# Sigmoid attention and a GELU feed-forward on one core: five decoder steps, sums ahead of a small read, parking tiles in the long-lived pool, a later x load

## The chip, the cores and the metric

The kernel runs on one core of one Trainium2 chip, as one program in one launch. The metric is the device time of that launch in microseconds, the median of three executions. TensorE (PE) multiplies, VectorE (DVE) and ScalarE (ACT) do the elementwise work, GpSimd (POOL) and SyncE (SP) issue DMA transfers, each in its own queue and in program order.

## The reference

The feed-forward's input is attention's output. Attention has 8 batches and 12 heads, a sequence of 448 and a head width of 64; the feed-forward is 3584 tokens, 768 to 2048 to 768.

```python
scores = scale * np.matmul(q, k.transpose(0, 1, 3, 2)) - np.log(S)
attn = 1.0 / (1.0 + np.exp(-scores))
out = np.matmul(attn, v)
...
h = x @ w_in
g = 0.5 * h * (1.0 + erf(h * inv_sqrt2))
return (g @ w_out).astype(np.float32)
```

q, k, v are float32. The weights w_in and w_out are drawn as float64 and reach the kernel as 64-bit words, so that the kernel itself makes float32 of them.

## The kernel before

**Attention** is a loop over 24 units `u`: 3 groups of two head pairs (four heads) for each of 8 batches. A unit makes its scores (six `sc` tiles and a tail), a sigmoid on ScalarE (`a`), and the values' product into one PSUM tile `pav` (function `values`). q and k are split into a rounded part and a remainder (`hi`, `lo`), three matmuls for a product. Half-way through `values`, VectorE makes a small read of `pav` (`mark`, L457), and the matmuls that come next into `pav` wait for that read. After it `meanwhile()` runs, and when the unit's values are complete `park` (L469) copies `pav` into an SBUF tile `x`, so that the PSUM banks can be used by the next unit's scores. Units 0 to 5 (the first two batches) store `x` by DMA into four SBUF tiles `x0`, the others into a DRAM scratch `scr_x`. The tile `x` belongs to the pool `at`, which lives as long as attention does.

**The decoder** (class `Decoder`) makes float32 of the weights, in 28 chunks: 16 of w_in, 12 of w_out. A chunk is loaded into `raw`, scaled by two ScalarE passes (L138, L141), finished by three VectorE instructions (L157, L160, L163) in `end`, and after every second chunk `post` makes the Strassen-Winograd sums: four of them for w_in (`mix`, L107 to L110) and seven stores to `scr_in`, or two for w_out (L182, L183) and five stores to `scr_out`. `work` is a generator in three steps a chunk: scale; end and the next load; post. Units 2 to 9, 11 to 18 and 20 to 23 take one step ahead of `values` and two in `meanwhile`. The rest of w_out is decoded in the first feed-forward layer of the first pair of batches.

**The feed-forward** takes the batches in four pairs `b`. `ffn1` has 56 products `n` (7 Winograd products times 8 blocks, 9 matmuls each), `ffn2` has 28 (18 matmuls each). The `late` pool opens when `at` closes and lies in the same SBUF space, so its first tiles (`h2`, `t4`, the `g` slots) must wait until the tiles of `at` are done with. Weight halves are staged by SP (`wst`), rounded on ScalarE (L265) and given a remainder by VectorE (L272). `X0_WORK` lists the products after which the first pair's own x operands are made. In `ffn2` of the first pair, each second product runs `mix_store(i)`: VectorE subtracts twice (`combine`, shown as L588), POOL stores two parts to `scr_out` and then loads the parts for `i+2` (L835) into one of two `wd` tiles; there are six such rounds. At product 4 of `ffn2`, POOL also gets eight loads of the next pair's x (L297).

Of the kernel before, what the change touches and what calls it, by code (L numbers as in the profile page):

```python
# [17 lines left out]
P = 128  # L18
# [4 lines left out]
def tile_sigmoid_attention_gelu_ffn(  # L23
# [88 lines left out]

    def square(m):
        return m.rearrange("p (h f n) -> p h f n", h=2, f=2)

    class Decoder:
        def __init__(self):
            self.raws, self.parts, self.out = {}, {}, None
            self.done = self.groups = self.closed = 0
            self.mixing, self.pending, self.pool = [], [], None  # L120
            self.steps = self.work()
            self.taken = 0
# [10 lines left out]
        def scale(self, i):  # L133
            w = CHUNKS[i][1]
            me = sb.tile([P, KC * S], U32, tag="me", name=f"me{i}", bufs=2)
            self.parts[i] = top = me[:, :w]
            half = self.raws[i].bitcast(I16)[:, : 4 * w].rearrange("p (n t) -> p n t", t=4)
            nc.scalar.activation(  # L138
                top.bitcast(F32), half[:, :, 2], AF.Prelu, bias=-LEAST, scale=-1.0, alpha=TINY
            )  # L140
            nc.scalar.activation(  # L141
# [8 lines left out]
        def end(self, i):  # L150
            _, w, kind, group, at = CHUNKS[i]
            words = self.raws.pop(i)[:, : 2 * w].rearrange("p (n t) -> p n t", t=2)[:, :, 0]
            top = self.parts.pop(i)
            if at == 0:
                self.out = sb.tile([P, 4 * QUAD], F32, tag="wd", name=f"wd{i}", bufs=2)
            bits = self.out[:, at : at + w].bitcast(U32)
            nc.vector.scalar_tensor_tensor(  # L157
                bits, words, 13, top, op0=ALU.logical_shift_right, op1=ALU.bitwise_or
# [3 lines left out]
            )  # L162
            nc.vector.tensor_tensor(bits, bits, words, op=ALU.add)  # L163
            if at:
                (self.mixing if kind == "in" else self.pending).append((group, self.out))

        def post(self):
            while self.mixing:
# [9 lines left out]
            while self.pool and self.pending:  # L178
                (c, e), a = self.pending.pop(0)
                a11, a12, a21, a22 = (a[:, i * QUAD : i * QUAD + QUAD] for i in range(4))  # L180
                s2 = self.pool(f"s{c}_{e}")
# [4 lines left out]
                self.groups += 1  # L186

        def work(self):
# [17 lines left out]
        def to(self, steps):  # L206
            self.go(max(0, math.ceil(steps) - self.taken))
# [4 lines left out]
        def until(self, *need):  # L212
            while not self.has(*need):
                assert self.taken <= 3 * len(CHUNKS)
# [4 lines left out]
    STEPS = {u: (1, 2) for u in (*range(2, 10), *range(11, 19), *range(20, 24))}  # L219
# [100 lines left out]
    def attention(at, ps):  # L320
        raws, vals, parts, probs, pavs, xs = {}, {}, {}, {}, {}, {}
# [51 lines left out]

        def spare(at, name):
            t = at.tile([P, 2, S], F32R, tag="hi", name=name, bufs=3)
            return t.bitcast(F32).rearrange("p a s -> p (a s)")[:, :QUAD]
# [87 lines left out]
        def park(u, p):  # L464
            if u < 0:
                return
            if p == 0:
                xs[u] = at.tile([P, 2, S], F32, tag="x", name=f"x{u}", bufs=2)
            nc.vector.tensor_copy(xs[u][:, p], pavs[u][:, p])  # L469
            b, n = divmod(u, NU)  # L470
            if b < 2:
                j, c = divmod(2 * n + p, KC)
                for i in range(2):
                    dst = x0[j, i].bitcast(F32)[:, c, b * HT : b * HT + HT]
                    nc.gpsimd.dma_start(dst, xs[u][:, p, i * HT : i * HT + HT])
            elif p == 1:
                nc.gpsimd.dma_start(scr_x[:, 2 * n : 2 * n + 2, b * S : (b + 1) * S], xs.pop(u))
# [16 lines left out]
        for u in range(total):  # L494
# [10 lines left out]
            if u == total - 1:  # L505
                W.low_to(3)
                dec.pool = lambda name: spare(at, name)

            def meanwhile():
# [4 lines left out]
                if u == total - 1:  # L514
                    dec.pool = None
                if u == 10:
                    x01, x11, x00 = (x0[jk].bitcast(F32) for jk in ((0, 1), (1, 1), (0, 0)))
                    nc.vector.tensor_tensor(x01, x11, x01, op=ALU.subtract)
                    nc.vector.tensor_tensor(x6, x01, x00, op=ALU.add)
                if u == 19:  # L520
                    lo = x0[0, 0]
# [374 lines left out]
```

## Time and profile before

| | |
|---|---|
| median of 3 runs | 1065.76 us (1063.42 to 1066.15) |
| the profiled execution | 1064.18 us, its span 1062.1 us |
| PE busy | 1014.5 us, 96% of the span |
| DVE busy | 708.0 us, 67% |
| ACT busy | 681.2 us, 64% |
| POOL busy | 120.2 us, 11% |
| mean granted TensorE clock | 0.987 of full speed |
| DMA over the span | 194 GB/s |

The span runs from the first to the last instruction of the profiled execution; some 2 us of the device time lie outside it. Of PE a busy share says little by itself: what counts is where it waited and at which of its two clock levels it ran.

### The profile page before, as it was taken

The numbers are of one execution on the slowest core, as the hardware profiler recorded it, in microseconds if no ns is written. First come the engines' busy times: TensorE is split into PE (matmuls) and PEld (weight loads), VectorE is DVE, ScalarE is ACT, GpSimd is POOL, SyncE is SP. The second block draws the span as 40 slices with busy tenths as digits, with TensorE's granted clock in tenths as the row PEclk, the third lists the DMA queues.
The fourth block names the chain that finished last, engine by engine and source line by source line (L and its number), as shares of the span: only waits on it lengthen the run. The fifth ranks groups of instructions, "written<-read, shape, count | busy, mean of one in ns | idle before, by whom it ended". The sixth has DMA issues, their size and how long they took to land.

```text
span 1062.1 us, 16574 instructions
## 1 busy us (share of the span) xinstructions
PE 1014.5 (96%) x6406; PEld 910.0 (86%) x6406; DVE 708.0 (67%) x822; ACT 681.2 (64%) x935; POOL 120.2 (11%) x186
## 2 busy tenths in 40 slices
PE   9999999899599995999999999999999999999998
PEld 5655555555589995999999999999999999999998
DVE  3667676767577894867338886843688674368874
ACT  5877777776678664556666564676656557666653
POOL 1332121302121225101000000100000000000000
PEclk9999999999899998899999999999999999999999
DMA  9999899997686667656443444643444453334442
GB/s 278 298 334 314 281 303 322 311 323 232 210 303 223 196 196 254 215 161 207 140 133 107 134 145 139 201 158 119 131 127 141 143 169 122 116 98 129 136 141 67
DMA packets 85294, 205.94 MB, mean 194 GB/s; under 512 B 9760, under 2 KB 34624, under 8 KB 85216
## 3 DMA queue, kind: packets, MB, share of 16 engines
q1 hardware_dynamic: 71056, 158.53, 49.1%
q0 software_dynamic: 13856, 46.02, 12.2%
q8 instruction: 50, 0.82, 0.3%
q10 hardware_dynamic: 304, 0.34, 0.1%
q14 instruction: 28, 0.23, 0.1%
HBM read 160.82 MB, written 41.29 MB: 190 GB/s over the span
## 4 chain that ended last, share of the span: by engine, by line
PE 59%; DMA 2%; issue 1%; DVE 0%; POOL 0%; ACT 0%; SPq 0%; DVEq 0%; POOLq 0%; ACTq 0%
PE pf L548 59%; DMA scr_out<-a 1%; DMA a<-scr_out 1%; DVE whl L272 0%; POOL a L835 0%; DMA out_dram<-tmp 0%; DVE a L588 0%; DVE op L588 0%; ACT tmp L803 0%; ACT tmp L798 0%; SPq L747 0%; DVEq L588 0%; DVEq L272 0%; ACTq L798 0%; POOLq L835 0%
## 5 line engine op out<-in xcount | busy, mean ns | idle before, releaser
L548 PE MATMUL pf<-op,whl 128*128 128x448 f32 x2016 | 385.6, 355 | 11.2 <-DVE op L588 11.2
L548 PEld LDWEIGHTS pf<-op,whl 128*128 128x128 f32 x2016 | 383.4, 191 | 12.7 <-DVE op L588 11.9
L548 PE MATMUL pf<-xh_p,whl 128*128 128x448 f32 x1296 | 354.6, 354 | 3.8 <-ACT g L698 2.1
L265 ACT CAST whl<-wst 128x768 fp32r<-128x768 f32 x224 | 186.6, 833 | 216.1 <-PE pf L548 191.0
L272 DVE TENSOR_TENSOR whl<-wst,whl 128x768 fp32r<-128x768 f32 x224 | 213.5, 955 | 141.1 <-ACT whl L265 140.8
L548 PEld LDWEIGHTS pf<-xh_p,whl 128*128 128x128 f32 x1296 | 246.1, 190 | 5.6 <-ACT g L698 2.4
L548 PE MATMUL pf<-xl_p,whl 128*128 128x448 f32 x600 | 212.3, 354 | 0.0
L371 ACT ACTIVATE a<-sc 128x896 f32<-128x896 f32 x144 | 120.3, 927 | 44.2 <-PE sc L397 44.0
L430 PE MATMUL pav<-a,v 64*64 64x448 f32 x1296 | 132.4, 541 | 0.0
L588 DVE TENSOR_TENSOR op<-g,op 128x896 fp32r<-128x896 f32 x112 | 121.4, 1085 | 0.9 <-ACT op L598 0.9
L548 PEld LDWEIGHTS pf<-xl_p,whl 128*128 128x128 f32 x600 | 114.1, 190 | 0.2
L430 PEld LDWEIGHTS pav<-a,v 64*64 64x64 f32 x1296 | 52.2, 132 | 64.0 <-issue 40.7
L598 ACT CAST op<-g 128x896 fp32r<-128x896 f32 x112 | 104.8, 935 | 2.6 <-PE pf L548 2.6
L588 DVE TENSOR_TENSOR g<-g,g 128x896 f32<-128x896 f32 x64 | 69.4, 1085 | 0.0
L397 PE MATMUL sc<-lo,hi 64*128 64x448 f32 x276 | 53.0, 375 | 15.6 <-DVE x L469 15.6
L588 DVE TENSOR_TENSOR tmp<-pf,g 128x448 f32<-128x448 f32 x64 | 40.0, 625 | 31.8 <-PE pf L548 31.2
L397 PEld LDWEIGHTS sc<-lo,hi 64*128 64x128 f32 x276 | 27.1, 186 | 35.5 <-issue 31.5
L585 ACT ACTIVATE g<-tmp 128x448 f32<-128x448 f32 x64 | 40.2, 628 | 25.9 <-DVE tmp L588 25.7
L297 POOL DMA_DIRECT2D x<-scr_x x24 | 17.9, 756 | 299.0 <-ACT g L694 186.1
L363 DVE TENSOR_TENSOR lo<-qk,hi 128x896 fp32r<-128x896 f32 x46 | 50.1, 1089 | 1.1
L457 DVE COPY ones<-pav 128x2 f32<-128x2 f32 x23 | 3.7, 160 | 70.5 <-PE pav L430 70.5
L397 PE MATMUL sc<-hi,lo 64*128 64x448 f32 x276 | 49.8, 349 | 0.0
(75 smaller groups left out, 830.9 us busy)
## 6 DMA issues: line engine op xcount, KB each, us to landing
wst<-scr_in SPq DMA_DIRECT2D x112, 384.0 KB, 3.3
wst<-scr_out SPq DMA_DIRECT2D x112, 384.0 KB, 3.1
v<-v_dram SPq DMA_DIRECT2D x48, 256.0 KB, 8.3
raw<-w_in_dram SPq DMA_DIRECT2D x16, 767.8 KB, 5.5
raw<-w_out_dram SPq DMA_DIRECT2D x12, 1023.5 KB, 6.2
qk<-q_dram SPq DMA_DIRECT2D x23, 448.0 KB, 10.1
qk<-k_dram SPq DMA_DIRECT2D x46, 224.0 KB, 10.6
out_dram<-tmp SPq DMA_DIRECT2D x43, 224.0 KB, 2.1
```

The lines of the kernel that those rows point to most:

```text
L265: nc.scalar.copy(hl[:, 0], t)
L272: nc.vector.tensor_tensor(hl[:, 1], t, hl[:, 0], op=ALU.subtract)
L297: queue.dma_start(dst[:, :, a], src[:, :, a])
L363: nc.vector.tensor_tensor(lo, raw, hi, op=ALU.subtract)
L371: nc.scalar.activation(to, sc, AF.Sigmoid, bias=NEG_LOG_S, scale=SCALE)
L397: nc.tensor.matmul(sc[:, j], ks[rows(j), 1, keys], braid(qs[rows(j), 0]) if braided else qs[rows(j), 0], start=n == 0, stop=n == last,)
L430: nc.tensor.matmul(pav[rows(j), p], vals[u][half, p, j, c], a[p][half, j], start=not swap and c == order[0], stop=c == (order[-1], FULL - ...
L457: nc.vector.tensor_copy(mark, pav[:, :, 0])
L548: nc.tensor.matmul(bank, a, braid(m), **flags)
L585: nc.scalar.activation(straight(dst), unbraid(src), AF.Gelu)
L588: nc.vector.tensor_tensor(out, a, b, op=op)
L598: nc.scalar.copy(op[:, 0], src)
```

## The change

It has five parts.

The decoder now has five steps for a chunk: the first ScalarE pass (`scale`); the second (`place`); `post` for the chunk before; the first two VectorE instructions (`join`); the third one and the next load (`round`). Units 2 to 9 and 11 to 18 take three steps ahead of `values` and two in `meanwhile`, so that `post`, with w_in's four sums, stands ahead of the small read `mark`. Units 20 to 23 take (3,1), (4,1), (4,1) and (4,2) steps.

Two sets of VectorE passes over the first x tiles (at units 10 and 19) also move from `meanwhile` to a place ahead of `values`, and the last remainder of attention's weights moves from the start of unit 23 into its `meanwhile`.

`park` copies each half into its own tile `piece` of the pool `sb`, with three buffers, in the ring that the feed-forward's `tmp` tiles use; it stores each half by itself. `at` holds no parking tile any more. w_out's sums take their scratch from the same ring, so they no longer need a pool lent to them.

In the first feed-forward layer the decoder's steps go to the products 2 to 45 that are not in `X0_WORK`.

In `ffn2` of the first pair the next pair's x is loaded at product 13, not 4; the other pairs keep product 4.

```diff
+    def piece(name):
+        return sb.tile([P, QUAD], F32, tag="tmp", name=name, bufs=3)
...
-            while self.pool and self.pending:
+            while self.pending:
                 (c, e), a = self.pending.pop(0)
                 a11, a12, a21, a22 = (a[:, i * QUAD : i * QUAD + QUAD] for i in range(4))
-                s2 = self.pool(f"s{c}_{e}")
+                s2 = piece(f"s{c}_{e}")
...
             for i in range(len(CHUNKS)):
                 self.scale(i)
-                yield
-                self.end(i)
-                self.load(i + 3)
-                yield
-                self.post()
-                yield
+                yield True
+                self.place(i)
+                yield True
+                yield self.post()
+                self.join(i)
+                yield True
+                self.round(i)
+                yield True
+            yield self.post()
...
-    STEPS = {u: (1, 2) for u in (*range(2, 10), *range(11, 19), *range(20, 24))}
+    STEPS = {u: (3, 2) for u in (*range(2, 10), *range(11, 19))}
+    STEPS |= {20: (3, 1), 21: (4, 1), 22: (4, 1), 23: (4, 2)}
...
-            if p == 0:
-                xs[u] = at.tile([P, 2, S], F32, tag="x", name=f"x{u}", bufs=2)
-            nc.vector.tensor_copy(xs[u][:, p], pavs[u][:, p])
+            x = piece(f"x{u}_{p}")[:, :S]
+            nc.vector.tensor_copy(x, pavs[u][:, p])
...
-            elif p == 1:
-                nc.gpsimd.dma_start(scr_x[:, 2 * n : 2 * n + 2, b * S : (b + 1) * S], xs.pop(u))
+            else:
+                nc.gpsimd.dma_start(scr_x[:, 2 * n + p, b * S : (b + 1) * S], x)
...
-                    dec.to(done + (3 * len(CHUNKS) + 1 - done) * min(1, n / 42))
+                    if n in live:
+                        share = (live.index(n) + 1) / len(live)
+                        dec.to(math.ceil(done + (STEPS_IN_ALL - done) * share))
...
-                if b + 1 < NB and n == 4:
+                if b + 1 < NB and n == (4 if b else 13):
```

On VectorE, inside attention: the end of one unit before (`wd` is a decoded chunk pair, `sin` w_in's sums, `x` the parking tile).

```order
L157 SCALAR_TENSOR_TENSOR wd_718<-raw_467,me_819 128x768
L160 TENSOR_SCALAR raw_467<-raw_467 128x768
L163 ISA wd_718<-raw_467,wd_718 128x1536
L107 TENSOR_TENSOR sin_845<-wd_718 128x384
L108 TENSOR_TENSOR sin_845<-sin_845,wd_718 128x384
L109 TENSOR_TENSOR sin_845<-wd_718 128x384
L110 TENSOR_TENSOR sin_845<-wd_718,sin_845 128x384
L469 COPY x_879<-pav_822 128x448 x2
```

And the unit after it in the changed kernel, where L399 and L390 are the splits of the next unit's q and k, L489 is the small read and L500 the parking copy.

```order
L399 TENSOR_TENSOR lo_0_858<-qk_680,hi_0_857 128x896
L390 CAST hi_1_942<-qk_680 128x896
L399 TENSOR_TENSOR lo_1_943<-qk_680,hi_1_942 128x896
L107 TENSOR_TENSOR sin_949<-wd_722 128x384
L108 TENSOR_TENSOR sin_949<-sin_949,wd_722 128x384
L109 TENSOR_TENSOR sin_949<-wd_722 128x384
L110 TENSOR_TENSOR sin_949<-wd_722,sin_949 128x384
L489 COPY ones<-pav_961 128x2
L171 SCALAR_TENSOR_TENSOR wd_979<-raw_591,me_946 128x768
L179 TENSOR_SCALAR raw_591<-raw_591 128x768
L186 ISA wd_979<-raw_591,wd_979 128x1536
L500 COPY x_0_1007<-pav_961 128x448
```

The four sums stood between the decode and the parking copy; they now stand between the splits and the small read, one unit later.

On VectorE, at the end of attention and the first instructions of the feed-forward, before (L182, L183 are w_out's sums, the two L588 make `t4` and the remainder of `h2`).

```order
L163 ISA wd_2935<-raw_2703,wd_2935 128x2048
L182 TENSOR_TENSOR wd_2699<-wd_2699 128x512
L183 TENSOR_TENSOR s_0_3051<-wd_2699 128x512
L182 TENSOR_TENSOR wd_2935<-wd_2935 128x512
L183 TENSOR_TENSOR s_1_3059<-wd_2935 128x512
L469 COPY x_3067<-pav_3029 128x448 x2
L588 TENSOR_TENSOR x_1_3088<-x_10_110,x_p_114 128x1344
L588 TENSOR_TENSOR x_10_110<-x_10_110,x_0_3087 128x1344
L272 TENSOR_TENSOR whl_3109<-wst_2610,whl_3109 128x768
```

The same place now (L308 is the weights' remainder, L611 are the two former L588).

```order
L186 ISA wd_2981<-raw_2829,wd_2981 128x2048
L308 TENSOR_TENSOR whl_2994<-wst_2630,whl_2994 128x768
L500 COPY x_0_3099<-pav_3074 128x448
L500 COPY x_1_3102<-pav_3074 128x448
L611 TENSOR_TENSOR x_1_3122<-x_10_110,x_p_114 128x1344
L611 TENSOR_TENSOR x_10_110<-x_10_110,x_0_3121 128x1344
L308 TENSOR_TENSOR whl_3143<-wst_2632,whl_3143 128x768
L308 TENSOR_TENSOR whl_3166<-wst_2855,whl_3166 128x768
```

The four sums have left this place (one pair went to unit 22, one into the feed-forward), and one remainder pass has come in.

On POOL, in `ffn2` of the first pair, before (`a` are the mix tiles: L842 stores, L835 loads; L297 loads x).

```order
L842 DMA scr_out_0_99<-a_3983 512x1x128
L842 DMA scr_out_0_107<-a_3983 512x1x128
L835 DMA a_4127<-scr_out_1_98 128x4x128
L835 DMA a_4127<-scr_out_1_102 128x4x128
L835 DMA a_4127<-scr_out_1_106 128x4x128
L297 DMA x_00_4161<-scr_x 128x3x224 x2
L297 DMA x_01_4164<-scr_x 128x3x224 x2
L297 DMA x_11_4167<-scr_x 128x3x224 x2
L297 DMA x_10_4170<-scr_x 128x3x224 x2
L842 DMA scr_out_0_99<-a_4064 512x1x128
L842 DMA scr_out_0_107<-a_4064 512x1x128
L835 DMA a_4204<-scr_out_1_98 128x4x128
```

The end of the six rounds now (L866 stores, L859 loads, L333 loads x).

```order
L866 DMA scr_out_1_108<-a_4169 512x1x128
L859 DMA a_4299<-scr_out_1_98 128x4x128
L859 DMA a_4299<-scr_out_1_102 128x4x128
L859 DMA a_4299<-scr_out_1_106 128x4x128
L866 DMA scr_out_1_100<-a_4234 512x1x128
L866 DMA scr_out_1_108<-a_4234 512x1x128
L866 DMA scr_out_1_100<-a_4299 512x1x128
L866 DMA scr_out_1_108<-a_4299 512x1x128
L333 DMA x_00_4488<-scr_x 128x3x224 x2
L333 DMA x_01_4491<-scr_x 128x3x224 x2
L333 DMA x_11_4494<-scr_x 128x3x224 x2
L333 DMA x_10_4497<-scr_x 128x3x224 x2
```

The eight x loads stood in the middle of the rounds and now stand behind the last store.

## Rows read from the trace of the kernel before

**Rows 1.** Waits of PE, whole span: total us, times, longest.

```profile
PE sc L397 <- DVE x L469: 15.6, 11, 1.7
PE pf L548 <- ACT g L694: 12.4, 1, 12.4
PE pf L548 <- DVE op L588: 11.2, 2, 10.1
PE pf L548 <- ACT g L698: 2.1, 1, 2.1
PE pf L548 <- ACT g L700: 1.7, 1, 1.7
```

**Rows 2.** Windows of PE alone: stretch; length, busy (instructions), granted clock, DMA.

```profile
486.12:676.11 189.99, 189.99 (x1006) 1.00 0.48 146
278.00:284.00 6.00, 5.91 (x23) 0.73 0.21 67
307.00:314.00 7.00, 6.50 (x25) 0.76 0.70 223
425.00:434.00 9.00, 8.71 (x30) 0.64 0.89 303
```

**Rows 3.** Timeline of DVE in attention: start, length, instruction [idle before <- releaser].

```profile
86.60 0.16 DVE L457 COPY ones<-pav 128x2 f32<-128x2 f32 x1 [2.95 <-PE pav L430]
...
89.80 0.56 DVE L107 TENSOR_TENSOR sin<-wd 128x384 f32<-128x384 f32 x1
...
91.81 1.15 DVE L469 COPY x<-pav 128x448 f32<-128x448 f32 x2
...
247.14 0.16 DVE L457 COPY ones<-pav 128x2 f32<-128x2 f32 x1 [2.03 <-PE pav L430]
```

**Rows 4.** Waits of PE's weight loads, attention: total us, times, longest.

```profile
PEld pav L430 <- DVE ones L457: 6.9, 23, 0.3
```

**Rows 5.** Windows of attention: length, busy by engine, granted clock, DMA share, GB/s.

```profile
20.00:80.00 60.00, 56.68 (x576) 33.20 (x574) 38.12 (x58) 46.57 (x56) 20.24 (x36) 1.00 1.03 322
...
200.00:220.00 20.00, 18.35 (x188) 10.19 (x187) 13.59 (x22) 11.94 (x15) 4.09 (x7) 1.00 1.02 357
```

**Rows 6.** Line L477, the parking stores of units 6 to 23, 448 KB each.

```profile
DMA to landing us min/median/max: 6.5/8.1/9.5
```

**Rows 7.** Timeline of ACT, DVE and PE where attention ends.

```profile
274.06 1.31 ACT L846 CAST x<-x 128x1344 fp32r<-128x1344 f32 x1 [15.69 <-DMA scr_x<-x]
261.53 0.68 DVE L182 TENSOR_TENSOR wd<-wd 128x512 f32<-128x512 f32 x1
...
264.26 1.15 DVE L469 COPY x<-pav 128x448 f32<-128x448 f32 x2
274.03 1.56 DVE L588 TENSOR_TENSOR x<-x,x_p 128x1344 f32<-128x1344 f32 x1 [8.62 <-DMA scr_x<-x]
278.09 3.52 PE L548 MATMUL pf<-x,whl 128*128 128x448 f32 x9 [12.41 <-ACT g L694]
```

**Rows 8.** Page, costliest groups: count, busy us, mean ns, idle ahead.

```profile
L272 DVE TENSOR_TENSOR whl<-wst,whl 128x768 fp32r<-128x768 f32 x224 | 213.5, 955 | 141.1 <-ACT whl L265 140.8
```

**Rows 9.** Timeline of POOL in the first pair's second layer.

```profile
389.87 1.52 POOL L842 DMA_DIRECT2D scr_out<-a  x2
397.66 2.26 POOL L835 DMA_DIRECT2D a<-scr_out  x3 [6.27 <-issue]
399.91 5.96 POOL L297 DMA_DIRECT2D x<-scr_x  x8
...
416.41 2.26 POOL L835 DMA_DIRECT2D a<-scr_out  x3 [8.29 <-DMA scr_out<-a]
...
423.78 2.27 POOL L835 DMA_DIRECT2D a<-scr_out  x3 [3.60 <-issue]
```

**Rows 10.** Timeline of DVE there: the fourth and fifth mix.

```profile
404.92 1.29 DVE L588 TENSOR_TENSOR a<-a 128x512 f32<-128x512 f32 x2 [3.69 <-DMA a<-scr_out]
...
422.07 1.29 DVE L588 TENSOR_TENSOR a<-a 128x512 f32<-128x512 f32 x2 [10.12 <-DMA a<-scr_out]
```

More of the change, by code (lines that the diff above doesn't have):

```diff
@@ L135, in scale, with place @@
             me = sb.tile([P, KC * S], U32, tag="me", name=f"me{i}", bufs=2)
-            self.parts[i] = top = me[:, :w]
+            self.parts[i] = me[:, :w]
             half = self.raws[i].bitcast(I16)[:, : 4 * w].rearrange("p (n t) -> p n t", t=4)
             nc.scalar.activation(
-                top.bitcast(F32), half[:, :, 2], AF.Prelu, bias=-LEAST, scale=-1.0, alpha=TINY
-            )
+                self.parts[i].bitcast(F32),
+                half[:, :, 2],
+                AF.Prelu,
+                bias=-LEAST,
+                scale=-1.0,
+                alpha=TINY,
+            )
+        def place(self, i):
+            top = self.parts[i]
             nc.scalar.activation(
@@ L148, in scale, with words @@
             )
-        def end(self, i):
+        def words(self, i):
             _, w, kind, group, at = CHUNKS[i]
-            words = self.raws.pop(i)[:, : 2 * w].rearrange("p (n t) -> p n t", t=2)[:, :, 0]
-            top = self.parts.pop(i)
             if at == 0:
@@ L162, in end, with round @@
             )
+            self.rest[i] = bits, words
+        def round(self, i):
+            bits, words = self.rest.pop(i)
             nc.vector.tensor_tensor(bits, bits, words, op=ALU.add)
+            _, _, kind, group, at = CHUNKS[i]
             if at:
                 (self.mixing if kind == "in" else self.pending).append((group, self.out))
+            self.raws.pop(i)
+            self.load(i + 3)
         def post(self):
+            some = bool(self.mixing or self.pending)
             while self.mixing:
@@ L186, in post @@
                 self.groups += 1
+            return some
         def work(self):
@@ L206, in to @@
         def to(self, steps):
-            self.go(max(0, math.ceil(steps) - self.taken))
+            while self.taken < min(steps, STEPS_IN_ALL):
+                self.taken += 1
+                if not next(self.steps, None):
+                    steps += 1
         def has(self, *need):
@@ L213, in until @@
             while not self.has(*need):
-                assert self.taken <= 3 * len(CHUNKS)
+                assert self.taken <= STEPS_IN_ALL
                 self.go(1)
@@ L563, in tmp @@
             return piece(f"tmp{count['tmp']}")[:, :S]
-        def piece(name):
-            return late.tile([P, QUAD], F32, tag="tmp", name=name, bufs=3)
         def flush():
@@ L674, in ffn1 @@
             done = dec.taken
+            live = [n for n in range(2, 46) if IN_ORDER[n] not in X0_WORK]
             for n, (p, j) in enumerate(IN_ORDER):
```

46 lines of the change are left out of this document (23 added, 23 removed).

## The prediction, as it was put on record

> **What bounds the kernel now.** I read PE's waits over the whole span first [rows 1]. PE is the engine on which the end hangs: once the first pair of batches is done it never stops, and a pair takes 189.99 us for 1008 matmuls, 0.1885 us each, at full clock [rows 2]. So only what PE loses ahead of that can be won back. The list has five entries, and they fall into three places. In attention PE waits 15.6 us in 11 pieces for the parking copy. Where attention ends it waits once, 12.4 us. In the first pair's two layers it waits 2.1 and 1.7 us for ScalarE copies in the first and 11.2 us for VectorE in the second.
>
> Then I read the granted clock behind those waits, in windows of PE [rows 2]: after the 12.4 us wait PE runs at the lower of its two levels for a while (mean 0.73 of full speed over 6 us, so 6 × 0.27 = 1.6 us lost), after the 2.1 us wait likewise (7 × 0.24 = 1.7 us), and after the longest wait of the second layer (9 × 0.36 = 3.2 us). Waits and clock together are 15.6 + 12.4 + 1.6 + 3.8 + 1.7 + 11.2 + 3.2 = 49.5 us. With all of it gone the span would be 1062.1 - 49.5 = 1012.6 us.
>
> **Part one, the sums ahead of the small read.** In a unit with w_in's sums, VectorE does the small read at 86.60, decodes, begins the sums at 89.80 and can park only at 91.81: the four sums hold the parking copy back by 2.0 us [rows 3]. PE then waits up to 1.7 us for the bank [rows 1]. Now the sums run ahead of the small read, where VectorE sat idle 2.95 us until PE had got that far [rows 3]. 2.0 fits into 2.95. The parking copy comes 2.0 us earlier, which is more than the longest of the waits, so these waits go. In units 20 to 22 the third decode instruction moves into the next unit in the same way.
>
> What hides the sums is that idle time, and it is smaller in the last units: 2.03 us at 247.14 [rows 3], where one decode instruction and two w_out sums (about 1.2 + 1.4 us, taken as the row at 261.53 and its like) now stand. There the small read comes some 0.6 us late. PE's weight loads do wait for that read, at all 23 units, 0.3 us at the longest today [rows 4]; so one unit pays up to 0.6 us. I take 0.3.
>
> Two costs are not in the trace. First, the unit becomes shorter while its bytes stay. Attention ends near 278.09 - 12.41 - 27 × 0.1885 = 260.6 us [rows 7, 2], 10.9 us a unit; without the waits 10.2. The transfers ran at 322 GB/s with a DMA share of 1.03 from 20 to 80 us, and at 357 GB/s with 1.02 from 200 to 220 [rows 5]. The shorter unit needs 322 × 260.6 / 245 = 343 GB/s. That lies between the two rows. If 322 is what those kinds of transfer can reach, nearly none of the 15.6 us is won; if 357 is, all. Nothing waits for a load today (no DMA stands in rows 1), and loads are issued one to three units ahead, which covers a deficit for some units. I take 1.0 us.
>
> Second, the parking ring. The copy of a unit's second half reuses the tile of the previous unit's first half; between the two copies lie 10.2 + 0.6 us, of which 0.7 go by until the store is issued. So a store must land within about 10 us. Stores of twice the size landed in 6.5, 8.1 at the median and 9.5 us at most [rows 6]. It holds, but not by much. I take 0.3 us, between nothing and some 0.5 us in each of 20 units. The Trainium skill prices such a transfer differently (DMA: Bandwidth & Descriptors, section Anatomy of one DMA — SWDGE (gpsimd) path: about 2.0 us fixed plus bytes over 436 GB/s). By that the half would land in 2.5 us, an estimate from the page, the whole in 3.1, and the ring could never be late; the trace's 8.1 us for the whole says otherwise, and I follow the trace.
>
> Part one: -15.6 + 0.3 + 1.0 + 0.3 = **-14.0 us**.
>
> **Part two, the end of attention.** ScalarE stood 15.69 us and VectorE 8.62 us until the last parking store had landed, since the feed-forward's first tiles lie where the parking tile of `at` lay [rows 7]. With the tile outside `at` that wait has no object. The next thing late is found by adding up. PE runs out of work at 278.09 - 12.41 = 265.7. ScalarE needs 278.09 - 274.06 = 4.0 us from its copy of `h2` to the `g` copy for which PE waits; it can begin when attention's last matmul is done, near 260.6, and is done by 264.6. VectorE parked at 264.26, after four sums that began at 261.53 [rows 7]. Those 2.7 us are gone, and one remainder pass (0.96 us [rows 8]) has come in: parking begins at 262.5 and ends at 263.6. Then come `t4` and the remainder of `h2`, 1.56 us each: 266.8. So VectorE is late next, by 1.1 us. That is less than the waits of up to 1.7 us behind which the clock stayed at 1.00 [rows 1, 5].
>
> Part two: -12.4 - 1.6 + 1.1 = **-12.9 us**.
>
> **Part three, the decoder's steps in the first layer.** The number of ScalarE and VectorE instructions stays the same, but no step falls on a product with x work any more. The two waits of 2.1 and 1.7 us [rows 1] were for ScalarE copies. Whether they stood behind such a pile I take from the code's order alone; and one pair of w_out sums more lies here now. Bounds: nothing gained, or 3.8 + 1.7 = 5.5 us. I take the middle: **-2.7 us**.
>
> **Part four, x later.** At 399.91 POOL issues eight x loads, 5.96 us of issue time, ahead of the next mix store, and their bytes then compete with it: the load behind that store goes out only at 416.41 [rows 9]. VectorE waits 10.12 us for it [rows 10] and PE 10.1 [rows 1]. With the loads behind the last round this goes. But POOL's own chain stays: a store, its landing, the next load. From one load's issue to the next it took 2.26 + (397.66 - 389.87) = 10.0 us, and later, with little else in flight, 423.78 - 416.41 = 7.4 us [rows 9]. VectorE wants a mix every 36 matmuls, 6.8 us. So the chain is slower than its consumer, and something stays.
>
> The load of round four goes out at 397.66 either way; the next two at 405.1 to 407.7 and 412.4 to 417.7. From a load's first issue to VectorE's start there passed 422.07 - 416.41 = 5.7 us [rows 9, 10]. So the mixes can start at 403.4, at 410.8 to 413.4 and at 418.1 to 423.4. Without waits VectorE would come to them at 404.92 - 3.69 = 401.2, 408.0 and 414.8 [rows 10]. The largest delay is 3.3 to 8.6 us. PE has a reserve: VectorE's 3.69 + 10.12 = 13.8 us of waiting cost PE 11.2, so 2.6 us are covered. PE loses 0.7 to 6.0 us, say 3.4, and 0.6 of clock (between none and 1.7). The x loads themselves have until the second layer's end, over 40 us after product 13 (13 × 18 × 0.1885 = 44).
>
> Part four: -11.2 - 3.2 + 3.4 + 0.6 = **-10.4 us**.
>
> **Sum.** -14.0 - 12.9 - 2.7 - 10.4 = -40.0. The profiled execution's span goes from 1062.1 to 1022.1; 2.1 us lie around it (1064.18 - 1062.1), so 1024.2. That execution lay 1.6 us under the median of the runs, within their spread of 2.7. I predict **1025 us**.
>
> **Rivals.**
>
> *The transfers bound attention.* For it: the DMA share of 1.03 over 60 us [rows 5]. Against it: 357 GB/s in another stretch, and no wait of PE for a load. If 322 GB/s is the ceiling, the unit stays at 10.9 us and part one gives perhaps 2 us: 1025 + 12 = 1037.
>
> *The mix chain, with its slow rounds, takes back most of part four.* For it: the 10.0 us round [rows 9]. Should each round take 10 us and the first layer give nothing either, 1025 + 2.6 + 1.1 + 2.7 = 1031.
>
> *The parking ring (the other side).* Stores land later as units get shorter, VectorE stands in the second half's copy, and PE waits for the bank as before, in every unit and not in 11. It begins to cost when a store takes over 10 us; slower than before it gets when some 23 units lose 1.8 us each (41 us), that is, when half-size stores take about 12 us all the time, against 9.5 at most for whole ones [rows 6]. At 11.5 us each, 23 × 1.5 = 34 us come back: 1059. At 12.2, about 1075.
>
> *The small read is late.* If the sums did not fit in 2.95 us, PE would stand at the second half of `values` and the 15.6 us would only change their place: 1025 + 14 = 1039. The fit of 2.0 into 2.95 speaks against it.
>
> **How the numbers follow.** Forecast 0.72, its own range 1016 (49.5 us less and 2.1 around it give 1014.7) to 1033 (all bounds against me: 1.3 more in attention, 2.7 in the first layer, 3.7 in the second). Transfers as the bound 0.11; the mix chain 0.09; the small read 0.04; the parking ring 0.04, of which half is slower than before. The range 1015 to 1037 leaves out the small read, the ring and part of the transfers' case, under 2 in 10. A measurement of this kernel tells no change from one of 0.3%, 3.2 us. Only the ring's case reaches that: faster 0.96, same 0.02, slower 0.02.
>
> **What would show it.** Right: no entry of some 15 us for the parking copy among PE's waits; ScalarE's first feed-forward copy near attention's last matmul; PE's first wait there near 1 us, with the clock at 1.00; in the second layer a wait of 1 to 6 us for VectorE and mix loads 7 to 10 us apart; x loads after the last mix store. Wrong: PE's weight loads waiting over 0.3 us for the small read in every unit; the parking copy waiting for a store; loads landing late with a DMA share above 1.03 and a rate no higher than 322; new ScalarE waits in the first layer.

## The result, and the profile after

The changed kernel takes 1022.45 us (median of three, 1020.52 to 1023.74) against 1065.76: a ratio of 0.9597 with a 95% interval of 0.9565 to 0.963. The forecast was 1025, with 1015 to 1037 around it. The profiled execution spans 1020.7 us against 1062.1, 41.4 us less. One execution of those that follow, of the whole of e7, took 1774.46 us at a granted clock of 0.556 and is left out of every comparison.

PE's waits over the whole span, after (engine, line, what is waited for: us in total, times, longest); they answer to [rows 1].

```profile
PE pf L574 <- DVE op L611: 5.6, 3, 3.2
PE pf L574 <- DVE x L611: 1.6, 1, 1.6
PE pf L574 <- ACT g L722: 0.8, 1, 0.8
PE sc L429 <- DMA qk<-k_dram: 0.3, 1, 0.3
PE sc L429 <- DVE x L500: 0.3, 1, 0.3
```

Of the eleven waits for the parking copy (now L500) one is left, of 0.3 us. The 12.4 us at the end of attention became 1.6. In the second layer 5.6 us of 11.2 stay. The places where PE passes from one stage to the next tell what each part was worth: its first feed-forward matmul starts at 242.64 us, before at 260.30 (17.7 us earlier); the first layer takes 98.6 us, before 115.7 (17.1 less); the first pair's second layer 103.4, before 110.1 (6.7 less). 17.7 + 17.1 + 6.7 = 41.5, the whole gain. How it splits is a matter of the execution too: in a second profiled one (e0 below) the same three gains are 15.6, 17.1 and 7.6 us.

**Attention.** VectorE's timeline, one unit of the changed kernel (start, length, line, operation; in brackets the idle time before it and what ended it), beside [rows 3]:

```profile
69.81 0.55 DVE L107 TENSOR_TENSOR sin<-wd 128x384 f32<-128x384 f32 x1
...
71.34 0.55 DVE L110 TENSOR_TENSOR sin<-wd,sin 128x384 f32<-128x384 f32 x1
72.80 0.16 DVE L489 COPY ones<-pav 128x2 f32<-128x2 f32 x1 [0.91 <-PE pav L462]
73.43 0.96 DVE L171 SCALAR_TENSOR_TENSOR wd<-raw,me 128x768 uint32<-128x768 uint32 x1 [0.46 <-ACT me L152]
...
75.89 1.15 DVE L500 COPY x<-pav 128x448 f32<-128x448 f32 x2
```

The sums took up 2.0 us of the idle time ahead of the small read L489, of which 0.91 us is left, and the parking copy comes 3.1 us after the small read and not 5.2. The windows of the same kernel (stretch, length, busy time of each engine with its count, granted clock, DMA share, GB/s), beside [rows 5]:

```profile
40.00:80.00 40.00, 40.00 (x410) 24.69 (x412) 29.75 (x45) 34.20 (x42) 15.65 (x29) 1.00 1.02 340
160.00:200.00 40.00, 40.00 (x412) 24.70 (x411) 30.87 (x45) 31.00 (x38) 10.36 (x18) 1.00 1.02 350
```

PE has no gap, and the transfers run at 340 to 350 GB/s with the same share of 1.02.

**The end of attention.** From the timelines of ScalarE, VectorE and PE, beside [rows 7]:

```profile
242.75 1.32 ACT L870 CAST x<-x 128x1344 fp32r<-128x1344 f32 x1 [1.32 <-DMA raw<-w_out_dram]
245.47 1.15 DVE L500 COPY x<-pav 128x448 f32<-128x448 f32 x2
246.53 1.55 DVE L611 TENSOR_TENSOR x<-x,x_p 128x1344 f32<-128x1344 f32 x1
248.19 1.56 DVE L611 TENSOR_TENSOR x<-x,x 128x1344 fp32r<-128x1344 f32 x1
249.80 1.78 PE L574 MATMUL pf<-x,whl 128*128 128x448 f32 x8 [1.60 <-DVE x L611]
```

ScalarE begins when PE's first feed-forward matmul has just started (242.64); its 1.32 us of idle time before that are put down to a weight load and cost PE nothing, since VectorE is ready later. VectorE is late next, with the remainder of `h2`, and PE waits 1.6 us for it.

**The second layer.** POOL's timeline there, beside [rows 9] (L859 is a mix's load, L866 its store, L333 x):

```profile
363.45 2.27 POOL L859 DMA_DIRECT2D a<-scr_out  x3 [6.87 <-issue]
365.71 1.52 POOL L866 DMA_DIRECT2D scr_out<-a  x2
371.97 2.27 POOL L859 DMA_DIRECT2D a<-scr_out  x3 [4.74 <-issue]
374.23 1.52 POOL L866 DMA_DIRECT2D scr_out<-a  x2
380.97 2.27 POOL L859 DMA_DIRECT2D a<-scr_out  x3 [5.22 <-DMA scr_out<-a]
...
391.03 6.15 POOL L333 DMA_DIRECT2D x<-scr_x  x8
```

The x loads come last now, but the loads of the mixes are still 8.5 and 9.0 us apart (10.65 before the first one shown) where VectorE wants one every 6.8 us. PE's timeline shows the price, three waits:

```profile
373.36 7.08 PE L574 MATMUL pf<-op,whl 128*128 128x448 f32 x36 [1.15 <-DVE op L611]
381.76 7.08 PE L574 MATMUL pf<-op,whl 128*128 128x448 f32 x36 [1.32 <-DVE op L611]
392.00 8.19 PE L574 MATMUL pf<-op,whl 128*128 128x448 f32 x33 [3.16 <-DVE op L611]
```

A window around the longest of them, beside the last of [rows 2]:

```profile
390.00:398.00 8.00, 6.00 (x23) 5.63 (x24) 8.00 (x10) 1.15 (x3) 7.19 (x10) 0.79 0.93 282
```

Behind that wait PE runs for a while at the lower of its two levels, which pulls the mean to 0.79 and costs 8 × 0.21 = 1.7 us. In the second execution (e0) the three waits are 6.4 us and the clock stays at full.

### The profile page after: what moved, and what is told of

It is laid out like the page before. It is cut to its first block, busy times and chain, and to the rows that moved or that the text cites. A ratio compares the mean times of both kernels' runs of the same rounds, so it can differ in the third digit from the quotient of the medians.

```text
span 1020.7 us, 16598 instructions
## 1 busy us (share of the span) xinstructions
PE 1007.5 (99%) x6406; PEld 909.4 (89%) x6406; DVE 704.1 (69%) x822; ACT 680.8 (67%) x935; POOL 129.7 (13%) x204
## 4 chain that ended last, share of the span: by engine, by line
PE 61%; DMA 2%; issue 0%; POOL 0%; DVE 0%; ACT 0%; SPq 0%; DVEq 0%; ACTq 0%; POOLq 0%
PE pf L574 61%; DMA scr_out<-a 1%; DMA a<-scr_out 1%; POOL a L859 0%; DMA out_dram<-tmp 0%; DVE op L611 0%; DVE a L611 0%; POOL scr_out L866 0%; ACT tmp L827 0%; DVE whl L308 0%; ACT tmp L822 0%; SPq L771 0%; DVEq L308 0%; DVEq L611 0%; ACTq L822 0%
## 5 line engine op out<-in xcount | busy, mean ns | idle before, releaser
L308 DVE TENSOR_TENSOR whl<-wst,whl 128x768 fp32r<-128x768 f32 x224 | 213.7, 955 | 142.9 <-ACT whl L301 142.6
L611 DVE TENSOR_TENSOR op<-g,op 128x896 fp32r<-128x896 f32 x112 | 121.4, 1085 | 0.9 <-ACT op L621 0.9
L462 PEld LDWEIGHTS pav<-a,v 64*64 64x64 f32 x1296 | 55.3, 132 | 61.4 <-issue 33.8
L611 DVE TENSOR_TENSOR g<-g,g 128x896 f32<-128x896 f32 x64 | 69.4, 1084 | 0.0
L611 DVE TENSOR_TENSOR tmp<-pf,g 128x448 f32<-128x448 f32 x64 | 39.9, 624 | 29.6 <-PE pf L574 27.9
L333 POOL DMA_DIRECT2D x<-scr_x x24 | 18.1, 808 | 294.6 <-ACT g L718 188.5
L399 DVE TENSOR_TENSOR lo<-qk,hi 128x896 fp32r<-128x896 f32 x46 | 50.1, 1089 | 1.1
L429 PE MATMUL sc<-hi 64*128 64x448 f32 x276 | 48.8, 349 | 0.0
L171 DVE SCALAR_TENSOR_TENSOR wd<-raw,me 128x768 uint32<-128x768 uint32 (+1 forms) x28 | 30.0, 1072 | 22.0 <-ACT me L152 20.6
## 6 DMA issues: line engine op xcount, KB each, us to landing
raw<-w_out_dram SPq DMA_DIRECT2D x12, 1023.5 KB, 8.1
qk<-k_dram SPq DMA_DIRECT2D x46, 224.0 KB, 11.2
```

The costliest lines, as they stand in the source:

```text
L171: nc.vector.scalar_tensor_tensor(bits, words, 13, self.parts.pop(i), op0=ALU.logical_shift_right, op1=ALU.bitwise_or,)
L308: nc.vector.tensor_tensor(hl[:, 1], t, hl[:, 0], op=ALU.subtract)
L333: queue.dma_start(dst[:, :, a], src[:, :, a])
L399: nc.vector.tensor_tensor(lo, raw, hi, op=ALU.subtract)
L429: nc.tensor.matmul(sc[:, j], ks[rows(j), 1, keys], braid(qs[rows(j), 0]) if braided else qs[rows(j), 0], start=n == 0, stop=n == last,)
L462: nc.tensor.matmul(pav[rows(j), p], vals[u][half, p, j, c], a[p][half, j], start=not swap and c == order[0], stop=c == (order[-1], FULL - ...
```

## The experiments

Kernels that were timed together are compared with each other; else by their ratio to the kernel before in the same company.

**The sums put back behind the decode (e1).** In the changed kernel:

```diff
-                yield self.post()
                 self.join(i)
                 yield True
                 self.round(i)
                 yield True
-            yield self.post()
+                yield self.post()
...
-    STEPS = {u: (3, 2) for u in (*range(2, 10), *range(11, 19))}
-    STEPS |= {20: (3, 1), 21: (4, 1), 22: (4, 1), 23: (4, 2)}
+    STEPS = {u: (2, 3) for u in (*range(2, 10), *range(11, 19), *range(20, 24))}
...
```

> The changed kernel with one thing undone: the sums stand behind the decode again (two steps ahead of the values' product, three in its middle, the sums last), so that VectorE makes them between the decode and the parking copy. The parking tiles, the places of the other x passes and the rest stay changed. Theory (the place of the sums carried all of part one): the parking copy comes back among PE's waits with 10 to 16 us in some 10 to 20 pieces, attention ends 14 to 18 us later, and a piece costs about 0.15 us more than its row says; 1022.4 + 17 = 1039 us (1035 to 1043). Rival (part one's gain came in part from the halved parking tiles and the moved x passes): the parking copy's waits stay under 8 us and the time under 1031 us.

Measured: 1047.6 us (1043.66 to 1052.1), ratio 0.9839 (0.9796 to 0.9882), 25 us over the changed kernel and more than the 1035 to 1043 expected; PE's first feed-forward matmul at 263.28. Of its PE waits:

```profile
PE sc L427 <- DVE x L498: 16.8, 12, 2.5
PE pf L572 <- DVE op L609: 7.7, 3, 4.3
```

Windows of the same kernel:

```profile
40.00:80.00 40.00, 36.67 (x370) 20.52 (x370) 26.64 (x41) 31.01 (x37) 14.59 (x27) 1.00 0.98 319
243.00:246.00 3.00, 2.46 (x14) 2.49 (x16) 2.93 (x5) 0.92 (x1) 1.44 (x2) 0.61 0.98 333
246.00:249.00 3.00, 3.00 (x27) 1.37 (x28) 0.71 (x1) 2.71 (x3) 0.00 (x0) 0.82 1.03 393
```

The waits are back in twelve pieces, so the place of the sums carries part one (w_out's sums went back with w_in's); the rival falls. Attention is 20.6 us longer, 4.1 us more than the rows of its waits grew (16.8 - 0.3). Two things make that up. The wait of 2.48 us that ends at 243.54 (there a weight remainder, L306, stands ahead of the parking copy as well) is followed by the lower level, about 3 × 0.39 + 3 × 0.18 = 1.7 us. And a row counts a wait from the modelled end of the matmul before it, 0.35 us after its start, while in an unbroken stream the next one starts after 0.19: each break costs 0.16 us more than its row. From 40 to 80 us PE's two breaks cost 40 matmuls against the changed kernel's window, 3.9 us, where their rows say 1.68 + 1.65 (0.3 us each; a few records can be missing). Twelve breaks at 0.2 us are the remaining 2.4. The rest lies behind attention: the first layer takes 101.9 us and not 98.6 (3.4 more, with a wait of 2.3 us for VectorE at its start and the lower level behind it), the second 105.4 and not 103.4 (1.9 more, with 7.7 us of waits). Why they are longer was not followed up.

**The x load alone (e5), and undone (e2).** One line each, in the kernel before and in the changed one:

```diff
-                if b + 1 < NB and n == 4:
+                if b + 1 < NB and n == (4 if b else 13):
```

> The kernel before with one part of the change alone: the second pair's x is loaded at product 13 of the second layer, not 4. Theory (part four stands by itself): PE's waits for VectorE's mixes fall from 11.2 us to 4 to 7 us, and the time by what the two traces show for this layer, 6.7 us: 1065.8 - 6.7 = 1059 us (1056 to 1061). Rival (POOL's own chain of store, landing and load sets the mixes, and the x loads hardly matter): 1064 to 1066 us.

```diff
-                if b + 1 < NB and n == (4 if b else 13):
+                if b + 1 < NB and n == 4:
```

> The changed kernel with one part undone: the second pair's x is loaded at product 4 of the second layer again. Theory (the eight x loads ahead of a mix store delay the next mix load): PE's waits for VectorE in this layer rise from 5.6 us to 9 to 12 us, with a single one over 8 us, and the clock's loss behind it from 1.7 to about 3 us: 1022.4 + 6.7 = 1029 us (1026 to 1032). Rival (POOL's own chain sets the mixes): 1022 to 1024 us.

Measured: e5 1058.49 us, ratio 0.9935 (0.9909 to 0.9961), 6.4 us gained; e2 1031.18 us, beside 1022.61 of the changed kernel in the same company (1020.51 to 1029.37, e0 below), 8.6 us lost. PE's waits in e5:

```profile
PE pf L548 <- DVE op L588: 5.8, 3, 2.8
```

And in e2:

```profile
PE pf L574 <- DVE op L611: 11.0, 2, 10.0
```

POOL's timeline in e2:

```profile
365.39 2.26 POOL L859 DMA_DIRECT2D a<-scr_out  x3 [6.01 <-issue]
367.64 5.21 POOL L333 DMA_DIRECT2D x<-scr_x  x7
...
384.42 2.26 POOL L859 DMA_DIRECT2D a<-scr_out  x3 [8.35 <-DMA scr_out<-a]
```

A window of e2 behind its wait of 9.96 us, which ends at 392.91:

```profile
390.00:396.00 6.00, 3.09 (x8) 2.81 (x9) 6.00 (x8) 0.78 (x2) 3.78 (x5) 0.50 0.59 181
```

The part stands by itself. What it is worth is read from the second layer alone, since other stages vary between executions: 103.6 us in e5 against 110.1, a gain of 6.5; 109.6 in e2 against 103.4 and 102.5 in the changed kernel's two traces, a loss of 6.1 to 7.0. So it is worth 6 to 7 us. The rest of e2's loss is not this part's: in its trace attention is 2.6 us longer than in the first trace of the changed kernel, 0.6 longer than in e0's. In e2 the eight x loads stand ahead of a mix store, and the next mix load goes out 19 us behind the last, as in [rows 9]; the wait that follows leaves PE at its lower level.

The changed kernel once more, for the runs in its company:

> The changed kernel as it is, in the same company as the next three, whose differences are small. 1022.4 us (1020.5 to 1024).

Measured: 1022.61 us, ratio 0.9605 (0.9575 to 0.9636); the profiled execution spans 1021.8 us. It shows what varies without any edit. Attention is 2.1 us longer than in the first trace (PE's first feed-forward matmul at 244.70): near 38 us ScalarE stood 2.69 us until a part of k had landed, and one of PE's units took 11.2 us and not 9.9. The same load was late in e7's half (2.33 us) and e10 (3.13), and in e5 (4.20) and e11 (2.20), which have attention's old order. The second layer is 0.9 us shorter, though its waits are longer:

```profile
PE pf L574 <- DVE op L611: 6.4, 3, 2.6
376.92 7.08 PE L574 MATMUL pf<-op,whl 128*128 128x448 f32 x36 [2.65 <-DVE op L611]
```

The granted clock is 1.00 from 374 to 382 us, so this wait of 2.65 us was not followed by the lower level.

**The parking tiles alone (e6).** In the kernel before:

```diff
-            if p == 0:
-                xs[u] = at.tile([P, 2, S], F32, tag="x", name=f"x{u}", bufs=2)
-            nc.vector.tensor_copy(xs[u][:, p], pavs[u][:, p])
+            x = piece(f"x{u}_{p}")[:, :S]
+            nc.vector.tensor_copy(x, pavs[u][:, p])
...
-                nc.gpsimd.dma_start(scr_x[:, 2 * n : 2 * n + 2, b * S : (b + 1) * S], xs.pop(u))
+                nc.gpsimd.dma_start(scr_x[:, 2 * n + p, b * S : (b + 1) * S], x)
```

> The kernel before with one part of the change alone: the parking tiles (and w_out's scratch in the first layer) lie in the ring of the long-lived pool, and each half is stored by itself; the order of the sums, the decoder's steps and the x loads are as before. Theory (part two stands by itself): ScalarE's and VectorE's first feed-forward copies no longer wait for the parking stores; VectorE, which still makes two sums ahead of the last parking copies, has the remainder of h2 at about 268.5 us, PE wants it at about 267.8, so a wait near 1 us takes the place of the 12.4 and the 1.6 us of clock: 1065.8 - 13 = 1052.8 us (1050 to 1056). Attention's 15.6 us of waits for the parking copy stay as they are. Rival (the ring is late: the parking copy waits for a store): attention's waits grow by more than 3 us and the time stays above 1057 us.

Measured: 1062.86 us, ratio 0.998 (0.9964 to 0.9996): nearly nothing. Both theories miss. Attention's waits did not grow (15.4 us), so the ring is not late, and yet PE's wait at the boundary is still there. Its waits:

```profile
PE pf L550 <- ACT g L693: 11.1, 1, 11.1
```

ScalarE's and VectorE's timelines where PE waits:

```profile
272.74 1.31 ACT L845 CAST x<-x 128x1344 fp32r<-128x1344 f32 x1 [14.37 <-DMA scr_out<-s]
272.68 1.56 DVE L587 TENSOR_TENSOR x<-x,x_p 128x1344 f32<-128x1344 f32 x1 [7.26 <-DMA scr_out<-s]
```

The releaser has changed: not the parking tile's store to `scr_x`, but the store of `s` to `scr_out`. That is the scratch of w_out's sums, which in the last unit `spare` takes from a `hi` tile of `at`. The pool had two holders, the later of which lands 1.3 us before the other did.

**The scratch too (e9).** On top of e6:

```diff
-                dec.pool = lambda name: spare(at, name)
+                dec.pool = piece
```

> The kernel before with its parking tiles in the long-lived pool, as in the run before this one, and now the scratch of w_out's sums in the last unit too, which there still lay in a tile of attention's pool and was stored to scr_out. Theory (the boundary had two holders, the parking tile's store and the scratch's store, and the second one alone kept ScalarE and VectorE waiting for all but 1.3 us): ScalarE's copy of h2 starts near 260.6 us and not at 272.7, PE's wait of 11.1 us for g falls to 1 to 2.5 us for VectorE; 1062.9 - 10.5 = 1052.4 us (1050 to 1055). Rival (some third holder in that pool): the wait stays above 5 us and the time above 1057 us.

Measured: 1058.31 us, ratio 0.9933 (0.9916 to 0.9951), some 5 us better than e6 and short of the expected 10.5. The timelines of ScalarE, VectorE and PE:

```profile
260.41 1.32 ACT L841 CAST x<-x 128x1344 fp32r<-128x1344 f32 x1 [2.06 <-PE pav L444]
264.18 0.62 DVE L467 COPY x<-pav 128x448 f32<-128x448 f32 x1
269.23 0.62 DVE L467 COPY x<-pav 128x448 f32<-128x448 f32 x1 [4.43 <-DMA scr_out<-s]
273.04 3.36 PE L546 MATMUL pf<-x,whl 128*128 128x448 f32 x8 [7.17 <-DVE x L583]
```

A window around the end of PE's wait:

```profile
270.00:274.00 4.00, 0.96 (x3) 0.89 (x4) 3.90 (x4) 0.00 (x0) 0.55 (x1) 0.50 0.75 264
```

ScalarE is free, as expected: its copy follows attention's last matmul. But the second half's parking copy stood 4.43 us for the same store. Two scratch tiles had just taken two of the ring's three places and the first half's copy the third, so the second half had to wait until a scratch had been stored. PE waits 7.17 us for VectorE and then runs at its lower level.

**No sums ahead of the last parking copies (e11).** On top of e9; the two groups of sums are made in the first layer:

```diff
-    STEPS = {u: (1, 2) for u in (*range(2, 10), *range(11, 19), *range(20, 24))}
+    STEPS = {u: (1, 2) for u in (*range(2, 10), *range(11, 19), *range(20, 23))} | {23: (1, 1)}
...
-                dec.pool = piece
```

> The kernel of the run before last of this line (before, with parking tiles and w_out's scratch in the long-lived ring), and now no w_out sums at all in attention's last unit: the two groups that stood ahead of the last parking copies are made in the first feed-forward layer instead. Theory (in that run the ring itself was held: two scratch tiles took two of its three places just ahead of the parking copies, and the second copy had to wait 4.43 us until a scratch had been stored): both parking copies run near 261.6 us, t4 and the remainder of h2 follow at once and end near 266, PE's wait of 7.2 us falls under 1.5 us and its half-speed stretch behind it goes; 1058.3 - 9 = 1049.3 us (1047 to 1053). Rival (the ring is only a part of it: the stores of wd, the issue of DMAs on POOL or the x tiles' own stores keep VectorE or ScalarE waiting as well): a wait of 3 us or more stays, 1053.5 us or more.

Measured: 1051.89 us, ratio 0.9881 (0.9864 to 0.9897), 5.5 us better than e9 by the ratios. VectorE's and PE's timelines:

```profile
262.96 1.15 DVE L467 COPY x<-pav 128x448 f32<-128x448 f32 x2
264.03 1.55 DVE L582 TENSOR_TENSOR x<-x,x_p 128x1344 f32<-128x1344 f32 x1
265.68 1.56 DVE L582 TENSOR_TENSOR x<-x,x 128x1344 fp32r<-128x1344 f32 x1
291.83 3.73 PE L545 MATMUL pf<-x,whl 128*128 128x448 f32 x9 [4.03 <-ACT g L688]
```

At the boundary PE no longer waits at all: the theory holds there. 2.6 us of the expected gain are missing, and the trace names a wait that is new in this form: 4.03 us for a `g` copy at 291.83, with 2.6 us of clock lost behind it, where the run before had a wait of 2.0 for a later copy and no loss. ScalarE had stood 5.42 us for a weight load until 287.99 and had then made two decoder passes ahead of the copy. The four weight loads issued from 277.8 to 286.3 took 8.9 to 10.2 us to land, against a median of 3.2 over the whole run; two decoder loads of 1023.5 KB and five stores of w_out's parts were issued in the same stretch. That these held them up is not shown.

**The decoder's spread undone (e3).** In the changed kernel:

```diff
-                    if n in live:
-                        share = (live.index(n) + 1) / len(live)
-                        dec.to(math.ceil(done + (STEPS_IN_ALL - done) * share))
+                    dec.to(math.ceil(done + (STEPS_IN_ALL - done) * min(1, n / 42)))
```

> The changed kernel with one part undone: in the first feed-forward layer the decoder's steps are spread over all products up to 42 again, those with x work among them, in five-step form. Theory (decoder steps that fall on a product with x work made ScalarE late): PE's waits for ScalarE copies of g come back, from 0.8 us to 2 to 4 us, some with a stretch at the lower clock behind them: 1022.4 + 3 = 1025.5 us (1023.5 to 1028). Rival (the waits of before had to do with the three-step form or with the w_out sums that stood there): the waits stay under 1.2 us and the time within 1 us of the changed kernel's.

Measured: 1024.79 us (1024.27 to 1027.4), ratio 0.9624 (0.9601 to 0.9647), beside 0.9605 (0.9575 to 0.9636) of the changed kernel: by the time, no difference that can be told. PE's waits for ScalarE:

```profile
PE pf L574 <- ACT g L722: 2.1, 1, 2.1
PE pf L574 <- ACT g L724: 1.1, 1, 1.1
```

A window around the longer one, which ends at 278.17:

```profile
274.00:282.00 8.00, 5.91 (x22) 5.23 (x22) 7.90 (x9) 6.53 (x10) 1.45 (x2) 0.79 0.53 146
```

The wait of 2.1 us is back, in its old place and with the lower level behind it (8 × 0.21 = 1.7 us). 3.2 us of waits instead of 0.8, and 1.7 of clock: 4.1 us in this layer. In the second layer the waits for the mixes are 3.9 us and not the 6.4 of e0: PE comes later to a chain that does not follow PE. But the layer is only 1.1 us shorter than e0's, since 1.7 us of clock are lost behind its wait of 3.0 us. Attention is 1.4 us shorter in e3's trace, without the late load of e0's, so the time shows even less.

**More bytes in attention (e7, whole and half).** In the changed kernel, behind `load(u + 3)`; for the half, one of the two head pairs and a scratch of half the size:

```diff
+            if 2 <= u < 20:
+                b, n = divmod(u, NU)
+                nc.sync.dma_start(dummy[u], q[b, 2 * n : 2 * n + 2].rearrange("p r s -> r p s"))
```

> The changed kernel with one more transfer in each of 18 units of attention (2 to 19): 448 KB of q are copied to a DRAM scratch that nobody reads, issued by SP behind the unit's q and k loads. It adds work that the reference does not have. Question: how near the transfers are to being the bound, with a DMA share of 1.0 already. Theory (there is a reserve): the rate over 40 to 200 us rises from about 340 GB/s to about 380, PE's waits for loads stay under 2 us, and the time within 1021 to 1025 us. Rival (a share of 1.0 means that the transfers are at their limit): 18 x 0.459 MB at 345 GB/s are 24 us more; attention ends 15 to 24 us later with PE waiting for qk and v loads, 1037 to 1047 us.

> The changed kernel with 224 KB (0.229 MB) more to move in each of 18 units of attention, from q to a DRAM scratch that nobody reads, half of what the run with 448 KB moved (its runs lay 6 to 16 us above the changed kernel's). It adds work that the reference does not have. Theory (the transfers have a reserve of some 20 to 40 GB/s over the 340 that the changed kernel uses): the half still fits, 1022 to 1025 us, with PE waiting for loads under 2 us. Rival (the transfers are at their limit, so every byte costs): half of what the whole cost, 1026 to 1031 us, with PE waiting for qk or v loads.

Measured: the whole 1028.64, 1030.73 and 1039.05 us, ratio 0.97 (0.9649 to 0.9752), some 10 us over the changed kernel, which is neither theory's time; no trace of these three was kept. The half took 1023.37 us, ratio 0.9605 (0.9586 to 0.9625): nothing. Windows of the half:

```profile
20.00:80.00 60.00, 59.59 (x601) 37.29 (x600) 41.36 (x62) 48.57 (x59) 20.76 (x37) 1.00 1.03 338
140.00:200.00 60.00, 60.00 (x616) 36.81 (x609) 46.42 (x70) 48.77 (x60) 17.48 (x31) 1.00 1.02 365
```

PE stays busy (59.59 and 60.00 of 60 us) while the transfers move 338 and 365 GB/s; the changed kernel moved 333 and 349 in the same two stretches, at a share that already read 1.03 and 1.01. So there is a reserve that takes in 224 KB a unit. That 448 KB go beyond it is a guess: where the whole one waits is open.

**A third set of buffers for the mixes (e8), and t4 in pieces (e10).** In the changed kernel; the third set takes parts of the two `me` tiles, and the first three loads go out at products 50, 52 and 54 of the first layer:

```diff
-                    if n // 2 + 2 < 2 * KE:
-                        mix_load(n // 2 + 2)
+                    if n // 2 + 3 < 2 * KE:
+                        mix_load(n // 2 + 3)
```

> The changed kernel with a third set of buffers for the six mixes of the second layer (parts of the two me tiles, which nothing else uses there), so that a mix's load is issued three mixes ahead and not two, the first three in the first layer from product 50. Theory (what is left of part four is the chain of store, landing and load on POOL, longer than the time between two mixes): the waits of 5.6 us for VectorE and the 1.7 us of clock behind the longest go: 1022.4 - 7.3 = 1015 us (1013.5 to 1018). Rival (the loads themselves are slow, or something else is late in their place): waits of 3 us or more stay in that layer, 1019 us or more.

Measured: **1014.94 us**, 7.7 us under the changed kernel; ratio 0.9538 (0.951 to 0.9565). Of PE's waits in the feed-forward these are left:

```profile
PE pf L574 <- DVE x L611: 1.6, 1, 1.6
PE pf L574 <- ACT g L722: 0.8, 1, 0.8
```

A window over the mixes of the second layer:

```profile
340.00:400.00 60.00, 60.00 (x319) 59.98 (x318) 55.94 (x64) 37.06 (x53) 21.46 (x29) 1.00 0.87 281
```

PE has no gap there. The remaining term of part four was the chain of store, landing and load. On top of that, e10:

```diff
-        combine(t4.bitcast(F32), x0[1, 0].bitcast(F32), x6)
-        combine(x0[1, 0], x0[1, 0].bitcast(F32), h2)
+        for c in range(KC):
+            x = x0[1, 0][:, c]
+            combine(t4[:, c].bitcast(F32), x.bitcast(F32), x6[:, c])
+            combine(x, x.bitcast(F32), h2[:, c])
```

> The version with three sets of mix buffers, and where attention ends VectorE makes t4 and h2's remainder in three pieces each, by turns, so that the first piece of the remainder is there some 2 us after the last parking copy and not 3.1. Theory (PE's last wait at the boundary, 1.6 us, is for the whole remainder, of which its product wants a third at a time): the wait falls to about 0.5 us, 1014.9 - 1.1 = 1013.8 us, which the profile can show and the time hardly. Rival (six short passes cost more than two long ones, or ScalarE's g copy is late next): the wait stays at 1.3 us or more.

Measured: the wait fell to 0.7 us in two pieces, as expected. The time, 1016.33 us with a ratio of 0.9545 (0.9528 to 0.9563), can't tell it from e8. Both beat the changed kernel.

## Why the prediction was right, and where its terms were off

The sum was -40.0 us, the span shows -41.4. The mechanisms were right in the main, but that closeness is luck: in this trace two errors of 3.7 us cancel, and by e0's trace parts one and four would read -15.6 and -7.6.

- **Part one** was forecast at -14.0 and brought -17.7. The direction and the mechanism were right (e1). The sum took -15.6 from the rows of the waits, which count each of eleven breaks some 0.2 us short: 15.6 + 11 × 0.2 = 17.8. Of the three costs set against it (small read 0.3, transfers 1.0, ring 0.3) the first came, at about 0.2 us: PE's weight loads wait 7.4 us in all for the small read, before 6.9 [rows 4], once 0.8, in unit 22 where the prediction had put it, and there PE's next matmul started 0.93 us after the tail's first and not 0.75. The second did not come in this trace, but in e0 a late load cost PE's unit 1.3 us. The third did not come.
- **The transfers as the bound** fell: the changed kernel moves 340 to 350 GB/s without a gap on PE (its second trace has one gap of 0.75 us, at 332 to 341 GB/s, so a single late load is possible), and the half of e7 adds to it at no cost.
- **The parking ring** was never late in the changed kernel. Half-size stores landed in 5.6, 6.8 at the median and 8.2 us at most, inside the 10 us that the ring gives. The Trainium skill (DMA: Bandwidth & Descriptors, section Anatomy of one DMA — SWDGE (gpsimd) path) would put them at about 2.5 us, an estimate by its formula; the trace does not agree, as it did not for the whole ones. By either, the ring holds. But its mechanism is real: in e9 a tile of the ring held the copy for 4.43 us.
- **Part two** was forecast at -12.9 and brought -12.4 (12.4 and 1.6 of clock gone, 1.6 come): a wait of 1.6 us for the very remainder that was named, against 1.1 forecast, with the clock at full. Its argument was incomplete, though. "With the tile outside `at` that wait has no object" is false: e6 does just that and gains next to nothing, since w_out's scratch lay in `at` too. And with both outside (e9), the scratch holds the ring. The gain needs three things together: the parking tile outside, the scratch outside (e6), and no scratch of the sums in the ring whose store is still under way when the parking copies come (e9, e11); the change moves the sums to do that. The prediction named the earlier sums only for the 2.7 us that VectorE saves.
- **Part three** was forecast at -2.7 between 0 and -5.5 and brought about -4.7: both waits went, the clock loss with them, and one wait of 0.8 us came. What was only read from the code's order, that these waits stood behind decoder steps on products with x work, is shown by e3 for the larger one.
- **Part four** was mis-sized: -10.4 forecast, -6.7 measured. The forecast left 3.4 us of wait and 0.6 of clock; there were 5.6 and 1.7, near the upper end of the bounds given (0.7 to 6.0 and none to 1.7), and in e0 6.4 and none. The rounds took 10.65, 8.5 and 9.0 us, where 7.4 to 10.0 had been assumed, and from a load's issue to VectorE's start 6.6 to 7.8 us passed, not 5.7. This was the rival of the mix chain, in half. That the chain is the cause is shown by e8.

## What to carry to other kernels

When a pool's end makes two engines wait, the row names only the holder that lets go last: list every tile of the pool that a late store still reads, and move all of them. A shared ring is held by whoever took it last, so a short-lived scratch just ahead of a copy that matters can bring back much of the wait (7.2 us in e9, after 11.1 in e6). Where a chain of store, landing and load is slower than its consumer, take the transfers in its way first (6 to 7 us here), and then give the chain one more buffer (7.7 us).

## What the runs showed of the hardware

- A DMA share of 1.0 was no ceiling on bytes: from 20 to 80 us attention ran at 1.03 with 322 GB/s before, at 1.03 with 333 in the changed kernel and at 1.03 with 338 in the half of e7; from 140 to 200 us the last two ran at 1.01 with 349 and at 1.02 with 365, with PE busy all the time.
- Behind waits of PE of up to 1.76 us the granted clock stayed at full, behind those of 2.76 us and more it was at the lower level for a while. In between both happened: waits of 2.06 (before), 2.09 (e3), 2.26 (e5), 2.32 and 2.48 us (e1) were followed by a loss of 1.6 to 1.7 us, waits of 2.00 to 2.01 (e5, e6, e9), 2.04 and 2.65 (e0), 2.19 (the half of e7) and 2.27 us (e1) by none. So the length of such a wait alone does not tell its price.
- In attention a broken stream cost about 0.2 us more than the row of its wait showed.
